# Batch 0 of a routed attention kernel in two rounds of 384 queries, keys and values kept on chip, some splits moved to GpSimd, matmuls on zeros in the first slots

## The chip, the cores and the metric

The kernel runs on one core of one Trainium2 chip. A core has five engines with a queue each: TensorE (PE; its weight loads are listed as PEld), VectorE (DVE), ScalarE (ACT), GpSimd (POOL) and SyncE (SP), which here only issues DMA transfers. Transfers run on 16 DMA engines that all queues share. The metric is the device time of one execution in microseconds; lower is better.

## The reference

Four batches, eight heads, 768 positions of 64 values; 16 centroids a head.

```python
q_n = q / (norm(q) + 1e-6); k_n = ...; c_n = ...
q_assign = argmax(einsum('bhsd,hcd->bhsc', q_n, c_n), -1)
k_assign = argmax(einsum('bhsd,hcd->bhsc', k_n, c_n), -1)
mask = q_assign[:, :, :, None] == k_assign[:, :, None, :]
scores = where(mask, q @ k^T / 8, -1e9)
attn = softmax(scores) @ v
x = attn.transpose(0, 2, 1, 3).reshape(3072, 512)
h = x @ w_in                      # 512 -> 2048
out = (h / (1 + exp(-h))) @ w_out # 2048 -> 512, float32
```

A query sees only the keys that were assigned to its own centroid. The heads' results side by side are the input of a two-layer projection.

## The kernel before

**One head.** `load_qk` and `load_v` (lines 69 to 82) bring a head's q, k and v in as float32, three transfers of 192 KB on SP's queue; POOL casts v into one half of a `vt` tile whose other half is ones, so that the product with `vt` also gives the softmax's sums. `hi` and `lo` (85, 93), both on DVE, split q and k into a float16 part and the float16 rest. `xpose` (101) turns both by DMA transposes into `ab`: 12 tiles (six of q, six of k) of 128 positions, with the high parts on partitions 0 to 63 and the rests on 64 to 127. `logits` (110) are eight matmuls with the centroids; `am_t`, `am_max`, `am_back` (124 to 143) find on DVE the largest of each position's 16 and leave a one-hot code, and `codes` (146) writes the codes, scaled, over partitions 64 to 79 of `ab`. The contraction over 80 partitions in `qk_mm` (158) then gives the score, and a large negative number where the codes differ.

**Slots.** The main loop (386 to 432) runs over the 32 heads i and, in each, over six tiles j of 128 keys. One pair i, j is called a slot here, numbered 6i + j, so that there are 192. In slot i, j PE does the scores of the next slot (768 queries against 128 keys), ACT takes `exp` of this one into `P`, and PE multiplies the head before with its v: `pv_mm` (173), half a pass of 384 queries at a time, three matmuls in each of j = 0, 1, 3, 4. `evac` (182) copies the sums out of PSUM on DVE. The normalization has four steps that are spread over the following two heads: `evac` sends the row of sums out as a small transfer that lays it over partitions (`zt`), `recip` (194) inverts it and writes it to DRAM (`rzd`), `bcast` (202) reads it back to 64 partitions (`rzb`), and `norm` (209), on POOL, multiplies and writes the head's rows of `xt`, the input of the projection.

**Projection.** It is cut in units: `unit_a` (225) is four matmuls for 128 of the 2048 hidden columns and 384 tokens, a tanh on ACT and a product on DVE into `gt`; `unit_aa` (243) is the same for 768 tokens; `unit_b` (267) is 16 matmuls of 512 columns for 128 tokens of output, a copy on DVE and a transfer out. A batch has 32 `unit_a` (or 16 `unit_aa`) and six `unit_b`. All heads of a batch have to be normalized before a `unit_a` of it can run. The batch before's 32 are put in the list `qa` in slot 63, 111 and 159 (head i with i % 8 == 2, j = 3). One is taken in each slot with j = 0, 1, 2, 4, and one `unit_b` in each with j = 5. What is left over, and the whole last batch, runs after the loop.

**What sets the order.** The order of instructions on each engine is the order of the program: nothing is rescheduled, and an engine that waits holds all that is behind it. Loads run ahead of their use by four to six heads. The weights come in eight transfers on POOL's queue (`w_load`, 291), each of which also turns float32 into float16; each is held back by `pace`, a copy on POOL of one column of a certain `P` (line 414). Those stand in heads 2, 4, 6 and 8 (`win_s`) and 9 to 12 (`wout_s`).

## Time and profile before

| | |
|---|---|
| time, median of 3 runs | 398.26 us (397.08 to 400.86) |
| the profiled execution's own time | 396.95 us |
| its span | 395.2 us |
| PE busy | 334.0 us (85%) |
| DVE busy | 264.4 us (67%) |
| ACT busy | 203.8 us (52%) |
| POOL busy | 99.0 us (25%) |
| DMA, hardware queues / POOL's queue | 46.6% / 7.2% of 16 engines' span |
| first exp | 16.1 us |
| first `unit_a` | 96.4 us |

All times in the profile are of one execution. A row of a timeline or a chain gives the start in us, the duration in us, the engine, the line and the operation; brackets give idle time ahead of it and what ended it. A row of a line's view gives the least, median and greatest duration in ns. SPq and POOLq are the engines' issuing of transfers, which isn't counted as busy. In the DMA issues the last number is the median time from issue to landing.

### The profile page before, as it was taken

The page shows a single profiled execution, that of the slowest core. Times are in us where ns is not written, and L with a number is a line of the kernel's source. Part 1 is how long each engine was busy: PE and PEld are TensorE (multiplying, and loading weights), DVE is VectorE, ACT ScalarE, POOL GpSimd, SP SyncE. Part 2 cuts the span into 40 slices and gives each one's busy share as a digit, 9 for nine tenths or more (in the row PEclk, how much of TensorE's full clock was granted, in tenths as well). Part 3 has the DMA queues.
Part 4 walks back from the last instruction along what each step waited for, and adds up shares of the span by engine and source line. Part 5 has one row for each costly group of instructions (what it writes and reads, how often), then busy time and mean ns, then how long its engine had stood idle before and what let it go on. Part 6 is the DMA issues. An engine that isn't in the chain of part 4 may idle for free.

```text
span 395.2 us, 5664 instructions
## 1 busy us (share of the span) xinstructions
PE 334.0 (85%) x1921; PEld 167.8 (42%) x1921; DVE 264.4 (67%) x590; ACT 203.8 (52%) x310; POOL 99.0 (25%) x148
## 2 busy tenths in 40 slices
PE   0539868977598799997999899979999999977995
PEld 0114433433254455553555455445555545443442
DVE  5959967876479977794788877786766345256421
ACT  4237746854376755573666666555657524044300
POOL 3110135454343222223221402260223105000000
PEclk9999978888599999999999999999999999999999
DMA  5695899999979835572555555544311103200022
GB/s 141 172 269 114 188 202 225 186 213 227 128 138 190 207 87 134 133 176 74 148 147 148 122 148 147 143 85 89 88 48 23 47 27 88 80 2 0 0 81 80
DMA packets 82125, 48.84 MB, mean 124 GB/s; under 512 B 62128, under 2 KB 76464, under 8 KB 82096
## 3 DMA queue, kind: packets, MB, share of 16 engines
q1 hardware_dynamic: 79408, 44.29, 46.6%
q0 software_dynamic: 2688, 4.19, 7.2%
q8 instruction: 15, 0.25, 0.3%
q14 instruction: 14, 0.11, 0.1%
HBM read 33.59 MB, written 6.39 MB: 101 GB/s over the span
## 4 chain that ended last, share of the span: by engine, by line
PE 61%; DVE 15%; DMA 12%; ACT 4%; issue 3%; POOL 2%; SPq 2%; ACTq 0%; POOLq 0%; DVEq 0%
PE po L271 21%; PE ph L232 13%; PE pO L177 12%; PE pS L162 7%; DMA vn<-in_v_dram 4%; PE pS L163 3%; PE phs L251 3%; DMA qk<-in_k_dram 3%; DVE osb L186 2%; DMA rzb<-rzd 2%; DMA zt<-osb 2%; DVE gt L261 2%; DVE gt L237 2%; PE psL L116 2%; DVE hl L90 1%
## 5 line engine op out<-in xcount | busy, mean ns | idle before, releaser
L169 ACT ACTIVATE P<-pS 128x768 f16<-128x768 f32 x192 | 148.1, 809 | 37.4 <-PE pS L163 37.2
L177 PE MATMUL pO<-P,vt 128*128 128x384 f16 x384 | 89.1, 344 | 14.0 <-DVE osb L186 13.9
L236 ACT ACTIVATE tn<-ph 128x384 f32<-128x384 f32 x96 | 47.2, 491 | 101.3 <-PE ph L232 96.2
L162 PE MATMUL pS<-ab 80*128 80x512 f16 x192 | 78.8, 410 | 15.5 <-DVE ab L153 9.2
L232 PE MATMUL ph<-xt,win_s 128*128 128x384 f16 x384 | 78.5, 328 | 9.8 <-POOL xt L213 9.8
L271 PE MATMUL po<-wout_s,gt 128*128 128x512 f16 x384 | 85.7, 379 | 0.0
L213 POOL TENSOR_TENSOR xt<-osb,rzb 64x384 f16<-64x384 f32 x64 | 65.1, 1035 | 49.7 <-DMA rzb<-rzd 48.7
L237 DVE SCALAR_TENSOR_TENSOR gt<-tn,ph 128x384 f16<-128x384 f32 x96 | 53.0, 553 | 35.8 <-ACT tn L236 34.0
L82 POOL CAST vt<-vn 128x384 f16<-128x384 f32 x32 | 18.0, 563 | 180.2 <-DMA vn<-in_v_dram 149.6
L177 PEld LDWEIGHTS <-vt 128*128 128x128 f16 x384 | 37.6, 101 | 58.9 <-issue 39.2
L271 PEld LDWEIGHTS <-gt 128*128 128x128 f16 x384 | 37.5, 98 | 43.6
L163 PE MATMUL pS<-ab 80*128 80x256 f16 x192 | 55.6, 289 | 0.0
L276 DVE TENSOR_SCALAR ot<-po 128x512 f32<-128x512 f32 x24 | 16.6, 692 | 52.3 <-PE po L271 52.3
L232 PEld LDWEIGHTS <-win_s 128*128 128x128 f16 x384 | 37.4, 97 | 26.7 <-issue 1.2
L186 DVE COPY osb<-pO 128x384 f32<-128x384 f32 x64 | 35.3, 551 | 3.2 <-PE pO L177 2.9
L96 DVE SCALAR_TENSOR_TENSOR hl<-qk,hl 128x768 f16<-128x768 f32 (+1 forms) x33 | 33.1, 1002 | 0.2
L162 PEld LDWEIGHTS <-ab 80*128 80x128 f16 x192 | 19.8, 103 | 29.0 <-DVE ab L153 10.3
L163 PEld LDWEIGHTS <-ab 80*128 80x128 f16 x192 | 19.8, 103 | 24.5 <-issue 12.8
L251 PE MATMUL phs<-xt,win_s 128*128 128x384 f16 x128 | 22.2, 327 | 5.2 <-DVE gt L261 5.2
L259 ACT ACTIVATE tn<-phs 128x768 f32<-128x768 f32 x16 | 13.0, 811 | 25.0 <-PE phs L251 25.0
L90 DVE TENSOR_SCALAR hl<-qk 128x768 f16<-128x768 f32 (+1 forms) x33 | 19.1, 580 | 8.7 <-DMA qk<-in_k_dram 5.5
L261 DVE SCALAR_TENSOR_TENSOR gt<-tn,phs 128x384 f16<-128x384 f32 x32 | 16.3, 551 | 12.1 <-ACT tn L259 12.1
(45 smaller groups left out, 175.7 us busy)
## 6 DMA issues: line engine op xcount, KB each, us to landing
qk<-in_q_dram SPq DMA_DIRECT2D x32, 192.0 KB, 3.4
qk<-in_k_dram SPq DMA_DIRECT2D x32, 192.0 KB, 3.2
vn<-in_v_dram SPq DMA_DIRECT2D x32, 192.0 KB, 3.7
rzb<-rzd SPq DMA_DIRECT2D x32, 192.0 KB, 3.9
out_dram<-ot SPq DMA_DIRECT2D x24, 256.0 KB, 2.2
win_s<-in_moe_w_in_dram POOLq DMA_DIRECT2D x4, 512.0 KB, 7.9
wout_s<-in_moe_w_out_dram POOLq DMA_DIRECT2D x4, 512.0 KB, 7.5
ab<-hl SPq DMA_TRANSPOSE x33, 3.8
```

Source lines behind the costliest of these rows:

```text
L96: nc.vector.scalar_tensor_tensor(out=hl[:, t, :, 1, :], in0=src[:, t], scalar=QS, in1=hl[:, t, :, 0, :], op0=ALU.mult, op1=ALU.subtract)
L162: nc.tensor.matmul(pS[:, 0:512], lhsT, ab[0:80, 0:4, :].rearrange("p n c -> p (n c)"), start=True, stop=True)
L163: nc.tensor.matmul(pS[:, 512:768], lhsT, ab[0:80, 4:6, :].rearrange("p n c -> p (n c)"), start=True, stop=True)
L169: nc.scalar.activation(out=P, in_=pst.pop((i, j))[:, 0:S], func=AF.Exp, bias=0.0, scale=ESC)
L177: nc.tensor.matmul(pOs[i], vts[i % NV][:, j, :], Ps[i, j][:, c * HALF : c * HALF + HALF], start=(j == 0), stop=(j == NJ - 1))
L186: nc.vector.tensor_copy(osb[:, c * HALF : c * HALF + HALF], pOs.pop(i))
L213: nc.gpsimd.tensor_tensor(out=xts[h // 2][o : o + 64, b * S + c * HALF : b * S + c * HALF + HALF], in0=osbs[i][o : o + 64, cs], in1=rzbs[i ...
L232: nc.tensor.matmul(ph, win_s[:, r, ts(fb, 128)], xts[r][:, T0 : T0 + HALF], start=(r == 0), stop=(r == NR - 1))
L236: nc.scalar.activation(out=tn, in_=ph, func=AF.Tanh, bias=0.0, scale=0.5)
L237: nc.vector.scalar_tensor_tensor(out=gt[:, fb, :], in0=tn, scalar=1.0, in1=ph, op0=ALU.add, op1=ALU.mult)
L251: nc.tensor.matmul(phs[:, 512 * c : 512 * c + HALF], win_s[:, r, ts(fb, 128)], xts[r][:, T0 : T0 + HALF], start=(r == 0), stop=(r == NR - 1),)
L271: nc.tensor.matmul(po, gt[:, fc, ts(t, 128)], wout_s[:, fc, :], start=(fc == 0), stop=(fc == NFB - 1))
```

## The change

Batch 0 is reordered; the later batches keep passes of one head.

- In the first 24 slots, four passes p = 0 to 3 each hold two heads, 2p and 2p + 1, with the first 384 queries: slots 0 to 2 of a pass take two key tiles each of the one head, slots 3 to 5 those of the other. In slots 24 to 47 passes 4 to 7 do the same for the other 384 queries. k (and the first half of q) of the eight heads stay in `abk0` to `abk7`.
- What was the loading, splitting, transposing and routing of one head is that of an *item*. Items 0 to 7 are one head's k and half of its q, nine tiles; items 8 and 9 are the other half of q of four heads each; items 10 to 33 are the heads of batches 1 to 3, twelve tiles.
- Each step of an item stands at a fixed distance from the slot that needs it (`due`, `at`). The steps before slot 0 are run in the order of negative slot numbers.
- `hi` moves from DVE to ACT for items 0 to 3 and to POOL for the others.
- `recip`, `bcast` and `norm` of batch 0's passes stand 3, 5 and 7 slots after the second evacuation, the others 5, 8 and 9 slots, as before.
- The first 16 `unit_a` of batch 0 are put in the list in slot 34, the other 16 in slot 58. In slots 48 to 95 they are taken at j = 1 and 4 alone. The other batches' are put in the list in slots 111 and 159, as before.
- The weights are gated by slots 3, 6, 9 and 12 (`win_s`) and 27, 33, 39 and 45 (`wout_s`).
- `xt` is held for two batches in place of four. `P` has 12 buffers (14), `osb` 3 (4), `rzb` 2 (3), `qk` and `vn` 4 (3).
- `fill` adds matmuls on a tile of zeros into a PSUM tile that nobody reads: 24 ahead of the first work on PE, 4 after the centroids' transpose, 2 in each slot below 34 that isn't a multiple of 3.
- The slots after 191 (to 204) are part of the same loop, where before a tail was written out by hand.

```diff
-    NV = 8
+    NSPLIT = H // 2
...
-    xts = [const.tile([128, NT], f16, name=f"xt{r}") for r in range(NR)]
-    vts = [const.tile([128, NJ, 128], f16, name=f"vt{n}") for n in range(NV)]
+    xts = [[const.tile([128, S], f16, name=f"xt{r}_{n}") for r in range(NR)] for n in range(2)]
+    vts = [const.tile([128, NJ, 128], f16, name=f"vt{n}") for n in range(H)]
...
+    zz = const.tile([128, 512], f16, name="zz")
+    items = [[(h, 0, 0), (h, 0, 3), (h, 1, 0)] for h in range(H)]
+    items += [[(h, 1, 3) for h in range(4 * n, 4 * n + 4)] for n in range(2)]
+    items += [[(hd, 0, 0), (hd, 0, 3), (hd, 1, 0), (hd, 1, 3)] for hd in range(H, NBH)]
+    NI = len(items)
...
+    def head_of(p, s):
+        return (2 * (p % NSPLIT) + s) if p < H else p
...
+    def hi(n, t=None, eng="pool"):
+        if n not in hls:
+            hls[n] = mp.tile([128, 12, 2, D], f16, name="hl", bufs=3)
+        ho, _, src = parts(n, t)
+        if eng == "act":
+            nc.scalar.activation(out=ho, in_=src, func=AF.Copy, bias=0.0, scale=QS)
+        else:
+            nc.gpsimd.tensor_scalar(out=ho, in0=src, scalar1=QS, scalar2=None, op0=ALU.mult)
...
+        if n < H:
+            ab = const.tile([128, 9, 128], f16, name=f"abk{n}")
+        else:
+            ab = mp.tile([128, 12, 128], f16, name="ab", bufs=5)
...
+        p, j = divmod(T, NJ)
+        pS = ps.tile([128, 1024], f32, name="pS", tag="st", bufs=2)
+        if p < H:
+            hd, a = head_of(p, j // 3), 3 * (p // NSPLIT)
+            for t in range(2):
+                nc.tensor.matmul(
+                    pS[:, 512 * t : 512 * t + HALF], k_tile(hd, 2 * (j % 3) + t)[0:80], q_tiles(hd, a, 3),
+                    start=True, stop=True,
                 )
-    @per_head
-    def qk_mm(i, j):
-        ab = abs_[i]
-        pS = ps.tile([128, 1024], f32, name="pS", tag="st", bufs=2)
-        lhsT = ab[0:80, NJ + j, :]
-        nc.tensor.matmul(pS[:, 0:512], lhsT, ab[0:80, 0:4, :].rearrange("p n c -> p (n c)"), start=True, stop=True)
-        nc.tensor.matmul(pS[:, 512:768], lhsT, ab[0:80, 4:6, :].rearrange("p n c -> p (n c)"), start=True, stop=True)
-        pst[i, j] = pS
-    @per_head
-    def exp(i, j):
-        P = mp.tile([128, S], f16, name="P", bufs=14)
-        nc.scalar.activation(out=P, in_=pst.pop((i, j))[:, 0:S], func=AF.Exp, bias=0.0, scale=ESC)
-        Ps[i, j] = P
-    @per_head
-    def pv_mm(i, c, js):
+        else:
+            lhsT = k_tile(p, j)[0:80]
+            nc.tensor.matmul(pS[:, 0:512], lhsT, q_tiles(p, 0, 4), start=True, stop=True)
+            nc.tensor.matmul(pS[:, 512:768], lhsT, q_tiles(p, 4, 2), start=True, stop=True)
+        pst[T] = pS
...
+        P = mp.tile([128, S], f16, name="P", bufs=12)
...
+    def pass_at(p, c):
+        return NJ * p + 3 * c + 3 if p < H else NJ * (p + 1) + 3 * c
...
+        rzb = mp.tile([128, S], f32, name="rzb", bufs=2)
+        rzd = rzds.pop(p)
+        if p < H:
+            for c in range(2):
+                cs = slice(c * HALF, c * HALF + HALF)
+                nc.sync.dma_start(rzb[64 * c : 64 * c + 64, cs], rzd[cs].unsqueeze(0).to_broadcast([64, HALF]))
...
+    def fill(n):
+        if n:
+            junk = ps.tile([128, 512], f32, name="junk", tag="mm", bufs=3)
+            for _ in range(n):
+                nc.tensor.matmul(junk, zz[:, 0:128], zz, start=True, stop=True)
...
+    nc.vector.memset(zz, 0.0)
...
+    at(-3, cast_v, 0)
+    nc.scalar.preload_act_table(AF.Sqrt)
+    fill(24)
...
+    hi(0, None, "act")
+    lo(0)
+    xpose(0)
...
+    fill(4)
...
+    def due(n):
+        if n < H:
+            return 3 * n - 1
+        if n < H + 2:
+            return NJ * (NSPLIT + 2 * (n - H)) - 1
+        return NJ * (n - 2) - 1
+    for n in range(NI):
+        d = due(n)
+        near = n < H + 2
+        at(d - 5, am_back, n)
+        at(d - 5, codes, n)
+        at(d - 6, am_max, n)
+        at(d - 7, am_t, n)
+        at(d - 8, logits, n)
+        if n > 0:
+            x = d - (14 if near else 17)
+            at(x, xpose, n)
+            at(x - 2, lo, n)
+            if n > 1:
+                at(x - 4, hi, n, None, "act" if n < 4 else "pool")
+        if n > 3:
+            at(d - (24 if near else 35), load_qk, n)
+    for hd in range(1, NBH):
+        T = 3 * hd if hd < H else NJ * hd
+        at(T - (12 if hd < H else 15), load_v, hd)
+        at(T - 6, cast_v, hd)
+    for n in range(2 * NR):
+        T = NJ * n // 2 + 3 if n < NR else NJ * (n + 1) - 3
+        def gated(T=T, n=n):
+            nc.gpsimd.tensor_copy(pace, Ps[T][:, 0:1])
+            w_load(n)
+        at(T, gated)
+    on_pe = (logits,)
...
+    pv_at, evac_at, ready = {}, {}, {}
+    for p in range(NBH):
+        for c in range(2):
+            T = pass_at(p, c)
+            pv_at[T] = (p, c, range(0, 3))
+            pv_at[T + 1] = (p, c, range(3, 6))
+            evac_at[T + 2] = (p, c)
+        E = T + 2
+        near = p < H or p == NBH - 1
+        at(E + (3 if near else 5), recip, p)
+        at(E + (5 if near else 8), bcast, p)
+        N = E + (7 if near else 9)
+        for c in range(2):
+            at(N, norm, p, c)
+        if p in (NSPLIT - 1, H - 1):
+            ready[N + 1] = [(0, p // NSPLIT)]
+        elif p % H == H - 1 and p < NBH - 1:
+            ready[N + 1] = [(p // H, 0), (p // H, 1)]
+    for T in range(min(steps), max(steps) + 1):
+        p, j = divmod(T, NJ)
+        if T in ready:
+            qa.extend((*r, fb) for r in ready[T] for fb in range(NFB))
+        qk_mm(T + 1)
+        for f, a in steps.get(T, []):
+            if f in on_pe:
+                f(*a)
+        if T >= 0:
+            wide = H <= p < 2 * H
+            if j in ((1, 4) if wide else (0, 1, 2, 4)):
                 pop_a()
             if j == 5:
                 pop_b()
-            if j in (0, 1):
-                pv_mm(i - 1, 0, range(3 * j, 3 * j + 3))
-            if j in (3, 4):
-                pv_mm(i - 1, 1, range(3 * j - 9, 3 * j - 6))
-            exp(i, j)
-            if j == 0:
-                am_back(i + 1)
-                codes(i + 1)
-                xpose(i + 3)
-                load_qk(i + 6)
-                load_v(i + 5)
-                if i >= 2:
-                    nc.gpsimd.tensor_copy(pace, Ps[i, 0][:, 0:1])
-                    if i % 2 == 0 or i > 2 * NR:
-                        w_load((i - 2) // 2 if i <= 2 * NR else i - NR - 1)
-            if j == 1:
-                hi(i + 5)
-                bcast(i - 3)
-            if j == 2:
-                evac(i - 1, 0)
-                norm(i - 3, 0)
-                norm(i - 3, 1)
-            if j == 3:
-                lo(i + 5)
-            if j == 4:
-                recip(i - 2)
-                am_t(i + 2)
-            if j == 5:
-                evac(i - 1, 1)
-                am_max(i + 2)
-            flush()
-    pop_a()
-    pv_mm(last, 0, range(NJ))
-    flush()
-    pop_a()
-    evac(last, 0)
-    pv_mm(last, 1, range(NJ))
-    recip(last - 1)
-    flush()
-    evac(last, 1)
-    bcast(last - 2)
-    bcast(last - 1)
-    norm(last - 2, 0)
-    norm(last - 2, 1)
-    pop_b()
-    recip(last)
-    flush()
-    bcast(last)
-    for i in (last - 1, last):
-        norm(i, 0)
-        norm(i, 1)
+            if T < 34 and T % 3:
+                fill(2)
+        if T in pv_at:
+            pv_mm(*pv_at[T])
+        exp(T)
+        for f, a in steps.get(T, []):
+            if f not in on_pe:
+                f(*a)
+        if T in evac_at:
+            evac(*evac_at[T])
+        flush()
```

## The prediction

> **What bounds the kernel now.** I read the busy time by stretch of 20 us first (columns: stretch, length, then busy us and instruction count of PE, PEld, DVE, ACT, POOL; granted clock; DMA share, where 1.00 is 16 busy engines; GB/s).
>
> ```profile
> 60.00:80.00 20.00, 17.55 (x108) 8.32 (x108) 16.59 (x40) 14.85 (x20) 8.96 (x11) 0.88 0.99 208
> 80.00:100.00 20.00, 13.55 (x70) 6.15 (x69) 12.24 (x29) 9.29 (x12) 10.81 (x14) 0.80 1.11 211
> 140.00:160.00 20.00, 20.00 (x123) 10.29 (x121) 14.72 (x36) 11.26 (x19) 5.13 (x8) 1.00 0.46 110
> 200.00:220.00 20.00, 19.54 (x124) 10.39 (x122) 16.64 (x36) 13.54 (x22) 5.25 (x8) 1.00 0.65 155
> ```
>
> From 140 us on PE is full. Before 100 us it is not, and the DMA engines are. The chain of work that ended last, cut to that early time, says what is waited for:
>
> ```profile
> 47.22 7.59 DMA zt<-osb
> 59.12 7.18 DMA qk<-in_k_dram
> 87.65 7.19 DMA vn<-in_v_dram
> 95.33 5.18 DMA vn<-in_v_dram
> ```
>
> Each was issued beside a weight load, whose row among the DMA issues gives the time to landing:
>
> ```profile
> win_s<-in_moe_w_in_dram POOLq DMA_DIRECT2D x4, 512.0 KB, 7.9
> ```
>
> The DMA view of 50 to 110 us prices both kinds of traffic in that 60 us:
>
> ```profile
> q1 hardware_dynamic: 18678, 9.13, 76.1%
> q0 software_dynamic: 1536, 2.76, 30.4%
> ```
>
> Software: 0.304 x 60 / 5 weight loads = 3.65 us of the engines each. Hardware: 0.761 x 60 / 8 heads = 5.7 us a head. Together 1.065 of capacity, so this stretch is DMA-bound.
>
> The ACT timeline shows the pace of slots (one exp each; I number slots 6 x head + j):
>
> ```profile
> 46.20 4.59 ACT L169 ACTIVATE P<-pS 128x768 f16<-128x768 f32 x6 [1.11 <-PE pS L163]
> 51.71 2.33 ACT L169 ACTIVATE P<-pS 128x768 f16<-128x768 f32 x3 [0.93 <-PE pS L163]
> 92.92 2.33 ACT L169 ACTIVATE P<-pS 128x768 f16<-128x768 f32 x3 [0.24 <-PE pS L163]
> 104.03 0.80 ACT L169 ACTIVATE P<-pS 128x768 f16<-128x768 f32 x1
> ```
>
> Undisturbed, a head without MoE work takes 51.71 - 46.20 = 5.51 us, and that is DVE: 0.555 (high part) + 0.953 (low part) + 0.546 + 0.343 + 0.358 + 0.575 (argmax) + 4 x 0.251 (codes) + 2 x 0.551 + 0.184 = 5.62. At 104.03 slot 65 starts, one late after a wait of PE's unit_a for xt (6.1 us). From here MoE work fills PE. Slot 96 starts at 152.1 and slot 111, head 18 j=3, at 177.9 by the same timeline.
>
> **The change part by part.** Every unit of work of the projections remains: 96 unit_a, 16 unit_aa, 24 unit_b. What moves is when batch 0's 32 unit_a start: before at slot 64 (first pop after slot 63's extend), now at slot 34, since four passes give the first 384 tokens of all 8 heads. They go on until slot 104, two per six slots in slots 48 to 95 (four elsewhere). From slot 111 on the pops fall in the same slots as before, except that one unit_b, previously after, now falls at slot 107: 3.46 us by its row. So what follows slot 111 costs 395.2 - 177.9 - 3.5 = 213.8 us, and the question is when slot 111 comes.
>
> *To slot 0.* Before 16.1 us. Now logits(2) precedes the first score matmul on PE, and it needs the third transpose. DVE ends the centroid copies at 10.7 in before; two low parts of 0.7 later, at 12.1, that transpose has its data, SP issues it behind two more loads (0.43 each) at about 13, and it lands 3.8 us later by its row, so slot 0 comes at about 18. The first four high parts go to ACT, between its rows of 0.491 (384 columns) and 0.809 (768), which lay idle until 16.14. The 24 zero matmuls begin at about 1.3. The trace has cold and warm rows for 512 columns:
>
> ```profile
> 16.90 0.61 PE L162 MATMUL pS<-ab 80*128 80x512 f16 x1
> 36.60 0.38 PE L162 MATMUL pS<-ab 80*128 80x512 f16 x1
> ```
>
> Start to start that is 0.42 against 0.22. Warm, 24 take 5.3 us and lie in front of the centroid transpose (9.7 us); cold they end at 11.5 and delay it by 1.8. I take 18 and keep 20. The Trainium skill ("TensorE: Matmul & The Clock Gate", Part 1) has the array at half rate until about 3.4 us of sustained work; by it 8 run cold, 16 warm, the end is at about 8.2 us and slot 0 stays at 18; the two rows agree in kind. Inside slots 0 to 33 two zero matmuls stand in two of three slots: 0.29 us a slot warm. PE's own slot is then 0.32 + 0.33 + 0.06 + 0.29 = 1.0 us, below what follows; without cover they cost 46 x 0.22 = 10 us, cold twice that.
>
> The exp of two halves of 384 has the row of the tanh of that shape (0.811 against 0.809), the score matmuls keep 768 columns, and the split loads and broadcasts keep their bytes: nothing.
>
> *Slots 0 to 33.* DVE: an item of nine tiles costs 0.953 x 0.75 + 0.546 + 0.343 + 0.358 + 0.575 + 3 x 0.251 = 3.29, its high part having gone to ACT (four items) and POOL; with about six items, three low parts more and four evacuations in slots 0 to 15, some 19 us there, then less than PE's 1.0 a slot: 18 + 19 + 18 = 55. DMA: K, V and half of Q of all heads, then the other halves, make 8 heads. Of a head's 5.7 us I give 0.9 to rzb (one of four equal 192 KB transfers) and the two small ones, an estimate; so 8 x 4.8 + 4 passes x 0.9 + about 4 for batch 1's first item = 46, plus four win loads, now gated by slots 3, 6, 9, 12, 14.6: 61 us. The first 20 us of before carry 0.63 x 20 = 12.6; the other 48 at 1.065 take 45.6. So slot 34 at 66, **DMA-bound**; bounds 58 (DVE and PE with some slack) and 72 (the 6.1 us wait for xt again: recip, bcast and norm have only 3, 2 and 2 slots, and POOL, SP and DVE each stand in order behind their wait). Before, slot 34 was at 60.4: this stage loses about 6.
>
> *Slots 34 to 50.* Three wout loads remain: per six slots 5.7 + 3.65 = 9.35, over 1.065 = 8.8 us; DVE needs 5.07 + 4 x 0.553 = 7.3. 17 slots: 21 to 25, I take 24. Slot 51 at 90 (before 78.1).
>
> *Slots 51 to 95.* A pass on DVE: 5.62 - 0.555 + 2 x 0.553 = 6.2; PE: the period of 10.6 us in the full stage,
>
> ```profile
> 141.19 3.46 PE po L271 x16
> 151.78 3.46 PE po L271 x16
> ```
>
> less 3.46 and four unit_a of 0.65 leaves 4.54, plus two unit_a 5.8. High parts on POOL are unseen in before. Below: nothing, DVE's 0.555 simply goes. Price on POOL: the cast of 384 columns 0.507, doubled 1.0; the product of two inputs, 0.994, doubled 2.0; I take 1.0, the one-input row. Either fits POOL's pass (1.0 + 0.5 + 2.0 of 6.6). What it does to DVE is the danger:
>
> ```profile
> L135 DVE TENSOR_TENSOR oh<-LT,mx x32: 357/358/1132, 13.4 to 299.6; 128x192 f16<-128x192 f32 x32
> L151 DVE TENSOR_SCALAR ab<-ohT x64: 250/251/1057, 14.4 to 300.9; 16x384 f16<-16x384 f16 x64
> ```
>
> The long ones lie beside POOL work. At worst one pass gains 0.77 + 4 x 0.81 + 0.66 (low part, 953 to 1609) = 4.7; medians are untouched with POOL at 0.25 to 0.5 busy. I take 0.4: 6.6 a pass. The skill ("GPSIMD Engine Reference", 4.1 and 8) speaks against the move: elementwise work belongs on VectorE, and instructions with two SBUF inputs contend with POOL; if that held every low part to its longest, 0.66 x 7.5 would add 5 us. Three of these passes carry a unit_b: PE 5.8 + 3.46 = 9.3. Sum: 4.5 x 6.6 + 3 x 9.3 = 58 (bounds 56 and 76). Slot 96 at 148 against 152.1.
>
> *Slots 96 to 110.* 7.3 + 6.7 + (3.46 + 2.3) = 20, before 25.8: at this point batch 0's projections are nearly done. Slot 111 at 168.
>
> In the full stage DVE has 5.07 + 4 x 0.553 + 0.69 = 8.0 of 10.6, so POOL's high parts may stretch it by 2.6 a head for nothing. Smaller rings (P 12 for 14, osb 3 for 4, rzb 2 for 3) are freed a slot or more before they are rewritten: nothing. The end: pops 9 and 2 in the slots after 191, norm of the last head some 19 us after them by its waits (2.0 + 2.8 + 3.9 landings, 2.0 norm, 9 to the second evacuation and the reciprocal), PE has 1.9 + 11 x 0.65 + 4 x 3.46 = 22.9 to cover it; if not covered, 3.
>
> **Sum.** 168 + 213.8 = 382 span. Around the span lie 396.95 - 395.2 = 1.75: 384. The profiled execution is 1.3 under the median of 398.26, which I compare with; one per cent (4 us, about what a measurement tells here) lies at 394.3 and 402.2.
>
> **Rivals.**
> 1. *The transfers overlap better than their sum.* DVE and PE pace alone: slot 34 at 58, 20 for the next 17, 56, 20, 213.8, 1.75: 369. For it: loads run 24 to 35 slots ahead. Against: 1.065 was the ceiling of 60 us.
> 2. *POOL's port takes DVE's gain.* At three of the 4.7 in the passes without unit_b (4.5 x 2.6 more), 1.5 in the others, and slot 34 at 70: 384 + 12 + 4 = 400 at most, 395 in the middle. For: the 1132. Against: the medians.
> 3. *Slower: the weights in front.* Eight loads fall in slots 3 to 45, where reads are densest and zt, rzd and rzb have least slack. If each holds everything for its 7.6 us to landing, not 3.65, eight x 3.95 = 32 come on top less what stalls hid already: 403 to 415. It decides from 5.9 us a load (18 us over). For: the four 5 to 7.6 us links of the chain. Against: the 46.7 us of slots 24 to 63 held four loads at a loss of about 11 in all.
> 4. *The change doesn't do what it says:* unit_a at slot 34 waits on xt and PE cools, or zeros leave the clock cold: 386 to 391, in the forecast's range.
>
> **Chances.** Forecast (376 to 392, with 4) 0.54; rival 1 0.14; rival 2 0.18; rival 3 0.14. Range 369 to 402: it takes in rivals 1 and 2. Faster by over 1%: 0.54 + 0.14 + a little of 2 = 0.70; within 1%: 0.15; slower: 0.15.
>
> **What would show it.** First unit_a at about 66, against 96; slot 111 at 168; DMA share near 1.0 until 90; the full stage at 10.6 a head. If slot 34 comes after 80 or a head in the full stage takes over 11, I am wrong.

## The result, and the profile after

The changed kernel takes **423.94 us** (median of 4 runs, 418.38 to 429.61), the one before 398.37 (397.08 to 400.86). The ratio, taken here and below over the executions within 1.5% of each kernel's fastest, is **1.0533**, 95% interval 1.0424 to 1.0643: some 5% slower, where 384 us were forecast. The profiled execution took 418.38 us, with a span of 416.2.

The starts of the slots (one `exp` each, from ACT's timeline) show where it went. "Rest" is what follows slot 111. The last four rows are kernels of the next section. Every row is one execution.

| us | slot 0 | 34 | 51 | 96 | 111 | rest | span |
|---|---|---|---|---|---|---|---|
| before | 16.1 | 60.4 | 78.1 | 152.1 | 177.9 | 217.2 | 395.2 |
| predicted | 18 | 66 | 90 | 148 | 168 | 213.8 | 382 |
| after | 17.4 | 76.8 | 106.6 | 171.5 | 193.2 | 223.0 | 416.2 |
| c2, five edits | 18.2 | 68.1 | 92.8 | 157.3 | 183.1 | 213.1 | 396.2 |
| c5, c2 with high parts on POOL | 18.6 | 71.6 | 101.2 | 167.6 | 194.2 | 213.2 | 407.4 |
| c7, c2 with short distances | 17.3 | 70.8 | 104.2 | 167.5 | 193.5 | 213.1 | 406.6 |
| c8, c2 with the early start | 18.6 | 68.9 | 99.6 | 168.9 | 191.5 | 221.1 | 412.6 |

Stage by stage, after minus predicted: -0.6 to slot 0, +11.4 in slots 0 to 33, +5.8 in 34 to 50, +6.9 in 51 to 95, +1.7 in 96 to 110, +9.2 in the rest; 34.4 in all.

First the busy time by stretch of the kernel after (columns as in the prediction):

```profile
40.00:60.00 20.00, 13.82 (x73) 6.70 (x73) 11.46 (x28) 8.46 (x11) 7.06 (x7) 0.83 0.65 154
60.00:80.00 20.00, 13.09 (x65) 6.24 (x64) 6.60 (x14) 8.26 (x11) 9.66 (x10) 0.83 0.72 137
200.00:220.00 20.00, 19.50 (x97) 9.48 (x97) 10.80 (x25) 8.79 (x15) 7.62 (x8) 0.85 0.31 73
```

From 40 to 80 us no engine is full and neither are the DMA engines (0.65 and 0.72; before they stood at 0.99 in both stretches). DVE, 15.8 and 16.6 of 20 us busy before, is now at 11.5 and 6.6. Nothing is the bound there: everything waits for something in turn. The last row looks full, but its clock of 0.85 says that PE works there for longer, not on more.

The chain of work that ended last, cut to 17 to 120 us, has these transfers among its pieces (start, duration, transfer):

```profile
33.80 5.92 DMA zt<-osb
41.62 6.71 DMA rzd<-rz
...
64.10 6.45 DMA zt<-osb
...
90.79 4.07 DMA rzd<-rz
```

They carry 1.5 and 3 KB; the median of `zt<-osb` from issue to landing is 2.4 us between 20 and 110 us, that of `rzd<-rz` 1.7. They are two of the links of the normalization. Before, both were slower there, 3.6 and 6.2 us by the median, but more slots stood between the steps. Of the loads of q, k and v, which took pieces of 5 to 7 us before, one piece of 2.42 us is left. DVE's timeline shows what stands behind one of them, and PE's what stands behind DVE:

```profile
70.57 0.19 DVE L273 RECIPROCAL rz<-zt 128x6 f32<-128x6 f32 x1 [5.02 <-DMA zt<-osb]
70.68 0.52 DVE L258 COPY osb<-pO 128x384 f32<-128x384 f32 x1
```

```profile
71.25 1.12 PE L252 MATMUL pO<-P,vt 128*128 128x384 f16 x3 [4.90 <-DVE osb L258]
...
77.33 0.65 PE L314 MATMUL ph<-xt,win_s 128*128 128x384 f16 x3
80.06 0.32 PE L314 MATMUL ph<-xt,win_s 128*128 128x384 f16 x1 [2.07 <-POOL xt L296]
```

The reciprocal stands on DVE ahead of the evacuation (L258); it waits 5.02 us for 1.5 KB, the evacuation with it, and PE 4.90 us for the bank. The last two rows are the first `unit_a`: three of its matmuls run at 77.33, the fourth waits for the norm of the last pass, with all of PE behind it. The same three waits over the whole run, in the table of waits of the kernel after (engine and line, releaser: us in all, times, longest):

```profile
POOL xt L296 <- DMA rzb<-rzd: 115.9, 22, 9.6
...
PE pO L252 <- DVE osb L258: 23.5, 19, 5.4
...
DVE rz L273 <- DMA zt<-osb: 18.0, 5, 5.2
```

Before:

```profile
POOL xt L213 <- DMA rzb<-rzd: 48.7, 11, 11.7
PE pO L177 <- DVE osb L186: 13.9, 15, 2.9
DVE rz L196 <- DMA zt<-osb: 8.0, 3, 3.4
```

POOL's part is on the page of the kernel after, among the busy times and the costliest groups:

```profile
PE 353.1 (85%) x1993; PEld 175.0 (42%) x1993; DVE 265.3 (64%) x567; ACT 205.0 (49%) x313; POOL 152.1 (37%) x156
...
L296 POOL TENSOR_TENSOR xt<-osb,rzb 64x384 f16<-64x384 f32 x64 | 63.8, 1010 | 168.4 <-DMA rzb<-rzd 115.9
...
L138 POOL TENSOR_SCALAR hl<-qk 128x768 f16<-128x768 f32 (+1 forms) x30 | 62.9, 2098 | 14.9 <-DVE ohT L190 8.9
```

A high part takes 2.1 us on POOL, where 1.0 was taken, and 0.555 on DVE before. DVE hardly waits for it in this kernel:

```profile
DVE hl L143 <- POOL hl L138: 1.8, 2, 1.0
```

PE's 353.1 us hold 24.2 us of zeros. Up to slot 111 PE is without work for some 41 us, before for 43 (the time to its first matmul and the gaps between them, from the trace): since the zeros now fill part of that time, useful work waits for longer than before.

### The profile page after: what moved, and what is told of

Its sections match the earlier page's. It is cut to its first block, busy times and chain, and to the rows that moved or that the text cites. A ratio compares the mean times of both kernels' runs of the same rounds, so it can differ in the third digit from the quotient of the medians.

```text
span 416.2 us, 5850 instructions
## 1 busy us (share of the span) xinstructions
PE 353.1 (85%) x1993; PEld 175.0 (42%) x1993; DVE 265.3 (64%) x567; ACT 205.0 (49%) x313; POOL 152.1 (37%) x156
## 3 DMA queue, kind: packets, MB, share of 16 engines
q0 software_dynamic: 2688, 4.19, 6.4%
## 4 chain that ended last, share of the span: by engine, by line
PE 48%; DMA 16%; DVE 16%; POOL 5%; SPq 5%; issue 5%; ACT 4%; POOLq 0%; DVEq 0%; ACTq 0%
PE po L353 18%; PE ph L314 10%; PE pO L252 8%; DMA rzb<-rzd 5%; DMA zt<-osb 5%; PE pS L220 4%; PE phs L333 3%; DMA rzd<-rz 3%; POOL hl L138 3%; DVE gt L319 3%; DMA abk<-hl 2%; POOL xt L296 2%; DVE ab L202 2%; PE pS L221 2%; SPq L108 2%
## 5 line engine op out<-in xcount | busy, mean ns | idle before, releaser
L296 POOL TENSOR_TENSOR xt<-osb,rzb 64x384 f16<-64x384 f32 x64 | 63.8, 1010 | 168.4 <-DMA rzb<-rzd 115.9
L252 PE MATMUL pO<-P,vt 128*128 128x384 f16 x384 | 88.0, 340 | 23.7 <-DVE osb L258 23.5
L353 PE MATMUL po<-wout_s,gt 128*128 128x512 f16 x384 | 88.1, 387 | 0.0
L138 POOL TENSOR_SCALAR hl<-qk 128x768 f16<-128x768 f32 (+1 forms) x30 | 62.9, 2098 | 14.9 <-DVE ohT L190 8.9
L220 PE MATMUL pS<-ab 80*128 80x512 f16 x144 | 56.0, 389 | 9.9 <-ACT P L235 9.3
L358 DVE TENSOR_SCALAR ot<-po 128x512 f32<-128x512 f32 x24 | 16.6, 691 | 58.8 <-PE po L353 58.8
L221 PE MATMUL pS<-ab 80*128 80x256 f16 x144 | 39.6, 275 | 0.0
L258 DVE COPY osb<-pO 128x384 f32<-128x384 f32 x64 | 35.0, 546 | 4.0 <-PE pO L252 4.0
L143 DVE SCALAR_TENSOR_TENSOR hl<-qk,hl 128x768 f16<-128x768 f32 (+1 forms) x34 | 30.5, 899 | 4.5 <-ACT hl L136 2.4
L377 PE MATMUL junk<-zz 128*128 128x512 f16 x72 | 24.2, 455 | 1.2 <-DVE zz L390 1.2
L221 PEld LDWEIGHTS <-ab 80*128 80x128 f16 x144 | 14.4, 100 | 23.4 <-issue 14.3
L343 DVE SCALAR_TENSOR_TENSOR gt<-tn,phs 128x384 f16<-128x384 f32 x32 | 16.3, 550 | 12.1 <-ACT tn L341 12.1
```

Source lines behind the costliest of these rows:

```text
L138: nc.gpsimd.tensor_scalar(out=ho, in0=src, scalar1=QS, scalar2=None, op0=ALU.mult)
L220: nc.tensor.matmul(pS[:, 0:512], lhsT, q_tiles(p, 0, 4), start=True, stop=True)
L221: nc.tensor.matmul(pS[:, 512:768], lhsT, q_tiles(p, 4, 2), start=True, stop=True)
L252: nc.tensor.matmul(pOs[p, c], vts[hd % H][:, j, :], rhs, start=(j == 0), stop=(j == NJ - 1))
L258: nc.vector.tensor_copy(osb[:, c * HALF : c * HALF + HALF], pOs.pop((p, c)))
L296: nc.gpsimd.tensor_tensor(out=xts[b % 2][h // 2][o : o + 64, T0 : T0 + HALF], in0=osbs[p][o : o + 64, cs], in1=rzbs[p][o : o + 64, cs], op ...
```

## The experiments

A diff is against the changed kernel unless it says otherwise, and expectations are as they were put down. Where two kernels ran on different chips, their ratios to the kernel before on the same chip are compared. Two theories stood at first: **A**, POOL's slow high parts hold it back; **B**, the normalization's steps stand too close together and each waits for a transfer that is late beside the weight loads.

### One cause at a time

**e1: the high parts on DVE.**

```diff
-            nc.gpsimd.tensor_scalar(out=ho, in0=src, scalar1=QS, ...)
+            nc.vector.tensor_scalar(out=ho, in0=src, scalar1=QS, ...)
```

> The changed kernel with one part undone: the high parts of items 4 to 33 are made on DVE again, not on POOL. Theory A (POOL): one high part takes 2.1 us on POOL, and there it stands between a norm, which waits for rzb, and the low part, whose transpose stands on SP ahead of the next rzb, so a head cannot go faster than that loop of some 10 us. Then slots 51 to 110 fall from 86.6 us to about 72 and what follows slot 111 from 223 to about 214: 423.9 becomes 400 to 406. Theory B (short chain beside weights): the loss sits in slots 0 to 50, where DVE stands before zt; nothing there changes, and DVE has 0.55 us more a head: 420 to 428.

416.69 us, ratio 1.0515 (1.0440 to 1.0591). Theory A alone falls: the ratio hardly moves (the two intervals leave room for some 6 us), and slots 51 to 95 take 63.8 us, in the kernel after 64.9. The chain of this kernel there is a round trip (start, duration, piece):

```profile
120.05 0.65 PE pO L252 x3
...
121.02 0.67 PE ph L314 x4
...
121.71 0.49 ACT tn L318
122.20 0.71 ACT P L235
122.91 0.54 DVE gt L319
123.45 0.47 DVE hl L138
123.92 0.48 DVE osb L258
...
124.44 0.65 PE pO L252 x3
```

`unit_a` at j = 1 and 4 stands just behind the half pass; its tanh and product come ahead of the evacuation, for which the next half pass waits: 4.39 us from one `pO` to the next, two to a head.

**e2: recip, bcast and norm of batch 0 at 5, 8 and 9 slots.**

```diff
-        near = p < H or p == NBH - 1
+        near = p == NBH - 1
```

> The changed kernel with batch 0's reciprocal, broadcast and norm at 5, 8 and 9 slots after the evacuation, as in the other batches, in place of 3, 5 and 7; the first unit_a then come in slot 36. Theory B: DVE's five waits for zt (18.0 us in all) lose about 2.5 us each, SP's waits for rzd vanish: slot 51 at about 94 in place of 106.6, 410 to 414 in all. Theory A: the loop through POOL decides from slot 51 on and is untouched, but the gain in front of it remains, so A alone gives 420 to 426 only if the early waits come back elsewhere.

423.46 us, 1.0664 (1.0578 to 1.0750). B alone falls as well: no gain.

**e7: the four `wout_s` loads in slots 52, 55, 58 and 61.**

```diff
-        T = NJ * n // 2 + 3 if n < NR else NJ * (n + 1) - 3
+        T = NJ * n // 2 + 3 if n < NR else 52 + 3 * (n - NR)
```

> The changed kernel with the four loads of the second weight gated by slots 52, 55, 58 and 61 in place of 27, 33, 39 and 45; the first unit_b needs them in slot 71. Theory B: zt and rzd of passes 3 to 7 no longer lie beside a weight load and land in about 2 and 2.8 us, not 4 to 6.5: slot 51 at about 95 in place of 106.6, of which the later loads take back up to 5 in slots 52 to 70: 412 to 418. Theory A: no change beyond that, slots 51 to 110 stay at 86 or more. If the loads cost their share wherever they stand, 422 to 426.

424.73 us, 1.0725 (1.0657 to 1.0793). Moving these four gains nothing. The three loads of slots 6, 9 and 12 stayed where they were.

**e11: all eight loads seven slots apart.**

```diff
-        T = NJ * n // 2 + 3 if n < NR else NJ * (n + 1) - 3
+        T = 3 + 7 * n
```

> The changed kernel with the eight weight loads seven slots apart, gated by slots 3, 10, 17, ... 52, in place of 3, 6, 9, 12 and 27, 33, 39, 45. Theory D: no three of them meet any more, the transpose and the small transfers beside them wait for one load (some 7 us to landing) and not for three: slot 51 at 95 to 100 in place of 106.6, 410 to 416. If it is the bytes and not their burst, slot 51 stays at 104 or more and the time at 419 to 425.

424.78 us, 1.0705 (1.0638 to 1.0772). Spreading them brings nothing by itself: slot 34 comes at 73.3, earlier than in the kernel after, but slots 34 to 50 then take 36.2 us, not 29.8.

**e10: no weight loads.** Both weights are constants that POOL writes (1.8 us each of the eight), so the projection is computed with other weights; the 4.19 MB are left out.

```diff
-            nc.gpsimd.dma_start(win_s[:, n, :], moe_w_in[ts(n, 128), :])
+            nc.gpsimd.memset(win_s[:, n, :], 0.01)
...
-            nc.gpsimd.dma_start(
-                wout_s[:, 4 * r : 4 * r + 4, :],
-                moe_w_out[512 * r : 512 * r + 512, :].rearrange("(c p) d -> p c d", p=128),
-            )
+            nc.gpsimd.memset(wout_s[:, 4 * r : 4 * r + 4, :], 0.01)
```

> The changed kernel without the eight weight loads: each is replaced by a fill of the same tile with a constant on POOL, some 2.2 us each, so the projections are computed with constant weights. Theory D (burst of weight loads): the loss in slots 0 to 50 comes from the 4.2 MB of weights, three of whose first four loads start within 6 us and hold the transfers queued behind them (transposes took 9 to 21 us to land there, 3.8 elsewhere). Then slot 51 comes at 80 to 88 in place of 106.6, and the time is 395 to 405. Theory B (the chain of normalization is too short by itself): zt and rzd still hold DVE and SP, slot 51 at 95 or later, 412 or more.

406.76 us, 1.0255 (1.0193 to 1.0317); slot 34 at 65.6, slot 51 at 95.6. The loads hold 11 us: by slot 51 (106.6 to 95.6), and by the ratios (0.028 of 396; the intervals allow 5 more or less). That is all of them, not just their place. With the same short distances DVE's waits for `zt` up to slot 34 shrink from 16.0 us to 4.0. But even with none, the kernel is 2.5% slower than the one before *with* its loads, and the head of the first `unit_a` (slots 30 to 35) takes 13.1 us.

**e3: no zeros.**

```diff
-    fill(24)
...
-    fill(4)
...
-            if T < 34 and T % 3:
-                fill(2)
```

> The changed kernel without any of the 72 matmuls on zeros (24 in front, 4 after the centroids, 44 in slots below 34), which nothing reads. Theories A and B both put the loss elsewhere: PE waits in those slots, so 421 to 426, or 2 to 4 slower if the clock stays at half rate longer. A third theory, C: the 24 in front and those in the slots delay PE's own work; then slot 34 comes 5 us or more earlier and the time is 414 to 419.

425.85 us, 1.0612 (1.0485 to 1.0739), an interval that covers the changed kernel's ratio: the zeros don't cost the loss, and whether they help is settled further down.

**e12: units of slots 48 to 95 at j = 2 and 5.**

```diff
-            if j in ((1, 4) if wide else (0, 1, 2, 4)):
+            if j in ((2, 5) if wide else (0, 1, 2, 4)):
```

> The changed kernel with the unit_a of slots 48 to 95 taken at j = 2 and 5 in place of j = 1 and 4. Theory E (round trip): in those slots a half pass is one round from PE over the tanh on ACT and the product on DVE to the evacuation, which stands behind that product on DVE and for which PE's next pass waits, 3.9 to 4.4 us each; with the product behind the evacuation the round is broken: slots 51 to 95 take 58 us in place of 64.9, 412 to 418. Theory A (POOL's loop of norm, high part, transpose and broadcast): no change, 64 or more there.

421.57 us, 1.0564 (1.0484 to 1.0644). Slots 51 to 95 take 60.1 us: the round trip was real, for some 4 us in that stage (60.1 again in c1 below, which has the same edit; 63.4 or more in all other single edits), but the total didn't follow.

**e13: the first 16 `unit_a` in slot 42.**

```diff
-            ready[N + 1] = [(0, p // NSPLIT)]
+            ready[N + 1 if p >= NSPLIT else 42] = [(0, p // NSPLIT)]
```

> The changed kernel with the first 16 unit_a of batch 0 put in the list in slot 42 in place of 34; nothing else moves. Theory F (the early start itself): in slot 34 PE stands in order before xt, whose chain of three small transfers and two waits needs some 15 us from the evacuation in slot 26, and eight slots are not that long; besides, batch 0's units then end at slot 104 and PE has nothing until xt of batch 1 (slots 105 to 112). Then slots 30 to 35 fall from 15.8 to about 9 us, the pause at slots 108 to 113 (14.8) to about 11, and the time from 423.9 to 411 to 416. If the wait is only moved, since DVE, SP and POOL stand before the same transfers: 420 or more.

417.08 us, 1.0521 (1.0459 to 1.0584). In the total a miss, but one term came in exactly: the rest after slot 111 is **213.1 us**, as predicted (213.8), not 223.0. What the 9.9 us are can be seen in PE's timeline of the kernel after,

```profile
195.99 0.65 PE L314 MATMUL ph<-xt,win_s 128*128 128x384 f16 x3
200.50 0.48 PE L314 MATMUL ph<-xt,win_s 128*128 128x384 f16 x1 [3.85 <-POOL xt L296]
...
202.37 5.40 PE L353 MATMUL po<-wout_s,gt 128*128 128x512 f16 x16
```

against that of e13:

```profile
203.59 3.62 PE L353 MATMUL po<-wout_s,gt 128*128 128x512 f16 x16
```

With the start in slot 34, batch 0's units run out at slot 104. The slots up to 111 then hold only attention, but for a `unit_b` in slot 107, and most pass in 0.8 us or so; the norm that batch 1's first `unit_a` needs stands a fixed number of *slots* behind, and comes 3.85 us late. PE has cooled by then: the granted clock is 0.67 from 202 to 208 us, 1.00 in e13 from 203 to 208, and `unit_b` takes 5.40 us in place of 3.62. Started eight slots later, the units reach as far as slot 112, and there is no gap.

### Together, and one taken back

**c1: e1, e11 and e12 together.**

```diff
-            nc.gpsimd.tensor_scalar(out=ho, in0=src, scalar1=QS, ...)
+            nc.vector.tensor_scalar(out=ho, in0=src, scalar1=QS, ...)
...
-        T = NJ * n // 2 + 3 if n < NR else NJ * (n + 1) - 3
+        T = 3 + 7 * n
...
-            if j in ((1, 4) if wide else (0, 1, 2, 4)):
+            if j in ((2, 5) if wide else (0, 1, 2, 4)):
```

> The three edits together: high parts on DVE, the weight loads seven slots apart from slot 3 on, and the unit_a of slots 48 to 95 at j = 2 and 5. If the parts add, 423.9 less 5 (measured for the high parts), 10 and 7: 400 to 404. If one of D and E is wrong, 410 or more.

413.81 us, 1.0442 (1.0365 to 1.0520). Not what was hoped for: the head of the first `unit_a` now takes 19.1 us.

**c2: the longer distances and the later start added, loads nine slots apart.** Against c1:

```diff
-        T = 3 + 7 * n
+        T = 3 + 9 * n
...
-        near = p < H or p == NBH - 1
+        near = p == NBH - 1
...
-            ready[N + 1] = [(0, p // NSPLIT)]
+            ready[N + 1 if p >= NSPLIT else 42] = [(0, p // NSPLIT)]
```

> High parts on DVE, weight loads nine slots apart (3, 12, ... 66), the unit_a of slots 48 to 95 at j = 2 and 5, batch 0's reciprocal, broadcast and norm at 5, 8 and 9 slots, its first unit_a in slot 42. If the four causes (POOL, weights, round trip, early start) add, as e10 and c1 let expect: slot 34 at 68, slot 51 at 93, slot 96 at 152, slot 111 at 178, 394 to 402: no slower than before. If there is a cost in the two rounds as such (nine-tile items, 1.5 times the transfers a slot), 406 or more.

**396.70 us** (10 runs), 1.0002 (0.9962 to 1.0041). The whole loss is gone. What is left of the change, the two rounds, keys and values on chip, the smaller rings and ACT's four high parts, neither gains nor costs in sum.

**c3: c2 without the zeros.** The diff is that of e3.

> The kernel c2 without any matmul on zeros. The zeros took 24.2 us of PE in the changed kernel. Theory C: some of that delays PE's own work: 4 to 8 us under c2. If PE waits for DVE and the transfers there anyway, within 3 us of c2.

395.83 us, 0.9994 (0.9961 to 1.0026): within the measurement the zeros bring and cost nothing. This is what e3 left open.

Then four of c2's five edits were taken back, each by itself.

**c5: the high parts back on POOL** (diff against c2).

```diff
-            nc.vector.tensor_scalar(out=ho, in0=src, scalar1=QS, ...)
+            nc.gpsimd.tensor_scalar(out=ho, in0=src, scalar1=QS, ...)
```

> The combination (396.7) with one of its edits taken back: the high parts of items 4 on are on POOL again. If the causes add, this one gives back its own share: DVE's stretches (26 us against 13 in all, a part of them on the path) and POOL's 2.1 us a part in the loop rzb, norm, cast, high part, low part, transpose: 401 to 405. If one cause hides behind the others and only all four gone makes the gain, it gives back nearly everything: 410 or more. If POOL's part costs nothing once there is distance between recip, bcast and norm: 395 to 399.

409.57 us, 1.0372 (1.0318 to 1.0427). Three timelines of c5 show one case. POOL:

```profile
77.74 2.06 POOL L296 TENSOR_TENSOR xt<-osb,rzb 64x384 f16<-64x384 f32 x2 [8.61 <-DMA rzb<-rzd]
79.89 2.13 POOL L138 TENSOR_SCALAR hl<-qk 128x768 f16<-128x768 f32 x1
```

DVE, whose low part needs that high part:

```profile
82.05 0.96 DVE L143 SCALAR_TENSOR_TENSOR hl<-qk,hl 128x768 f16<-128x768 f32 x1 [4.83 <-POOL hl L138]
...
83.58 0.55 DVE L258 COPY osb<-pO 128x384 f32<-128x384 f32 x1
```

And PE:

```profile
84.18 1.12 PE L252 MATMUL pO<-P,vt 128*128 128x384 f16 x3 [4.01 <-DVE osb L258]
```

The norm stands ahead of the high part on POOL and waits 8.61 us for `rzb`; the high part waits with it, the low part (L143) waits on DVE, the evacuation behind that, and PE 4.01 us for the evacuation. In c5's table of waits that is

```profile
DVE hl L143 <- POOL hl L138: 21.6, 7, 6.8
```

and c2, whose high parts are on DVE, has no such wait. The second cost is on DVE itself. The rows of the codes, c5's first,

```profile
L200 DVE TENSOR_SCALAR ab<-ohT x56: 250/254/1395, 45.2 to 312.5; 16x384 f16<-16x384 f16 x56
```

and c2's,

```profile
L200 DVE TENSOR_SCALAR ab<-ohT x56: 250/254/552, 47.5 to 301.5; 16x384 f16<-16x384 f16 x56
```

have the same medians and another longest. Summed over all lines, what DVE's instructions take beyond their line's median is 26.1 us in c5 and 12.1 in c2 (27.1 in the kernel after, 14.1 in e1, 13.5 before). So the 30 high parts save DVE about 16 us and their neighbours give some 14 of them back. How the loss, 14.7 us by the ratios, divides between the wait and the stretch is open.

**c6: the weights' gates back** (diff against c2).

```diff
-        T = 3 + 9 * n
+        T = NJ * n // 2 + 3 if n < NR else NJ * (n + 1) - 3
```

> The combination (396.7) with the weights gated again in slots 3, 6, 9, 12, 27, 33, 39 and 45. If the causes add: slot 24 later by 5 to 8 us than the combination's 52.4 (item 8's transpose lands beside three loads), slot 51 by 8 to 10, and 402 to 408. If hidden behind the others: 410 or more. If the weights' place is not a cause, as the three single trials of it would have it: 395 to 399.

398.18 us (10 runs, 390.71 to 405.17), 0.9947 (0.9887 to 1.0006). That ratio rests on the four fastest of the ten; the medians of all give 398.18 / 396.11 = 1.0052. Either way the place of the loads costs at most some 2 us once the other four edits are in; the spread is wide. One cost of theirs is still there: a transpose of 14.1 us, for which PE waits 6.0 us in slots 12 to 23 of the profiled execution. Slot 96 comes at 156.0 all the same (157.3 in c2).

**c7: the short distances back** (diff against c2).

```diff
-        near = p == NBH - 1
+        near = p < H or p == NBH - 1
```

> The combination (396.7) with recip, bcast and norm of batch 0's passes back at 3, 5 and 7 slots. DVE waits again for zt and POOL for rzb, about 5 us each time that a load or a transpose is beside it. If the causes add: slots 24 to 51 longer by 3 to 6 us and 400 to 404; hidden: 410 or more; no cause: 395 to 399.

409.02 us, 1.0246 (1.0154 to 1.0337; 1.0326 by the medians of all). In c7's DVE timeline

```profile
81.45 0.19 DVE L273 RECIPROCAL rz<-zt 128x6 f32<-128x6 f32 x1 [10.32 <-DMA zt<-osb]
```

and in PE's

```profile
82.14 1.12 PE L252 MATMUL pO<-P,vt 128*128 128x384 f16 x3 [9.21 <-DVE osb L258]
```

the reciprocal, two slots earlier than in c2, waits 10.32 us, and PE 9.21. In c2 no reciprocal between 50 and 110 us waited longer than 3.8 us.

**c8: the start of the units right behind the norm, here slot 36** (diff against c2).

```diff
-            ready[N + 1 if p >= NSPLIT else 42] = [(0, p // NSPLIT)]
+            ready[N + 1] = [(0, p // NSPLIT)]
```

> The combination (396.7) with the first 16 unit_a in the list right after the norm of pass 3 (slot 36 by the longer distances) and not in slot 42. PE then stands at the first unit_a, and batch 0's units run out by slot 106, so that heads 18 and 19 take 14 and 12 us (8.5 and 10.6 in the combination). If the causes add: slot 51 later by 2 to 6 us, what follows slot 111 220 in place of 213, sum 404 to 410. If only the early wait counts and the late gap is filled: 398 to 402.

412.46 us, 1.0388 (1.0314 to 1.0461). Both ends of it are there: the first `unit_a`,

```profile
70.91 0.65 PE L314 MATMUL ph<-xt,win_s 128*128 128x384 f16 x3
78.29 0.48 PE L314 MATMUL ph<-xt,win_s 128*128 128x384 f16 x1 [6.73 <-POOL xt L296]
78.56 1.17 PE L252 MATMUL pO<-P,vt 128*128 128x384 f16 x3
```

waits 6.73 us and leaves PE cold (1.17 us for three `pO`, 0.65 warm), and the rest after slot 111 is 221.1 us, near the 223.0 of the kernel after.

**What the set says.** Any one of three things, POOL's high parts, the short distances or the early start, put back into a kernel that ties costs 10 to 15 us by its ratio: some 40 us added up, where the whole loss is 21. And each one alone taken out of the changed kernel gives back 1 us or less by its ratio, with intervals that leave room for some 6. So they are not terms of a sum; they lengthen or tighten the same ring of waits, and while one is left, the ring stays late. This ring is argued from the chains of c5, c7 and c8; the runs show the counts. Two questions are without a measurement: c2 with the pops at j = 1 and 4 again, and c2 with every high part on ACT.

### The one part in the old order

**b1: the kernel before with the high parts of heads 5 to 31 on POOL.** Against the kernel before:

```diff
-        nc.vector.tensor_scalar(out=hl[:, t, :, 0, :], in0=src[:, t], scalar1=QS, ...)
+        (nc.gpsimd if i > 4 else nc.vector).tensor_scalar(out=hl[:, t, :, 0, :], in0=src[:, t], scalar1=QS, ...)
```

> The kernel before with one part of the change alone: the high parts of heads 5 to 31 on POOL (2.1 us each there) at the same places. Theory A's remainder, from e1 (5 to 7 us for 30 of them): 400 to 404, the loss in heads without unit_b and in the early heads, where DVE paces. If POOL's port costs nothing where PE is full and DVE's 0.55 a head pays in the early heads: 392 to 397.

**525.02 us**, 1.3238 (1.3167 to 1.3309): a miss by 120 us, and the most telling run. Its chain from 137 us on (start, duration, piece), one head:

```profile
137.81 4.21 DMA vn<-in_v_dram
142.17 0.50 POOL vt L82
142.78 0.83 issue
143.61 2.16 POOL hl L90
145.79 2.69 DVE hl L96
...
150.10 1.30 SPq L106
151.46 1.04 SPq L72
152.55 0.43 SPq L73
153.03 5.01 DMA vn<-in_v_dram
```

Three engines that each run in order close a ring. POOL's high part stands behind a cast that waits for a load of v; DVE's low part waits for POOL; SP's transposes (L106) wait for DVE; and the next load of v stands behind them on SP. The low part is slow as well: it takes 2.69 us beside the norm that follows the high part on POOL, where its median is 0.96:

```profile
L96 DVE SCALAR_TENSOR_TENSOR hl<-qk,hl x33: 558/959/2694, 4.4 to 390.5; 128x768 f16<-128x768 f32 x31, 128x384 f16<-128x384 f32 x2
```

Once around takes 153.03 - 137.81 = 15.2 us; a head takes 13.6 in slots 51 to 95 of b1 (102.3 us for seven and a half), and 9.9 before. `load_v` issues the load and its cast together, so that POOL always stands for the landing (149.6 us of it already before), which is free only as long as nobody waits for POOL. The arithmetic alone would be 2.16 us for 0.555, on an engine that was three quarters idle.

## Why the prediction was wrong

*To slot 0* held: 17.4 against 18. The first 24 zeros took 7.02 us, between 24 x 0.22 = 5.3 warm and 24 x 0.42 = 10.1 cold (in the slots there are 44 more, not 46). High parts on ACT take 0.68 us, between the 0.491 and 0.809 that bounded them.

***Slots 0 to 33* is the step that failed first.** It called the stretch "DMA-bound" and summed bytes, a weight load as 3.65 us: slot 34 at 66, bounds 58 and 72. It came at 76.8, past the bound, and at 75.9 to 84.3 in e1, e3, e7, e12 and e13, which have the same first four loads and the same distances. The DMA share is 1.05 from 20 to 40 us, as reckoned, but 0.65 and 0.72 in the next 40, so bytes don't set it. What the runs put in its place is when transfers land beside the loads: without the loads (e10) and with the same distances slot 34 comes at 65.6. The step had the right words for what waits, "recip, bcast and norm have only 3, 2 and 2 slots, and POOL, SP and DVE each stand in order behind their wait", and priced them once, at "the 6.1 us wait for xt again". They are paid every pass: transfers of 1.5 and 3 KB at 5 to 7 us, DVE behind them (3.9, 5.3, 1.9 and 5.0 us for `zt` in the four passes of this stretch), PE behind DVE. Nor did 5 or 8 slots help alone (e2): there DVE waits for `zt` once, 4.0 us, but a transpose takes 17.0 us beside the loads and PE waits 9.0 us for it.

*Slots 34 to 50* was 29.8 us, not 24, and the forecast again summed bytes. It holds the first `unit_a`. In c2, which starts them in slot 42 and has the other four edits too, it is 24.7; in c8, c2 with the early start, 30.7.

*Slots 51 to 95* was 64.9, not 58, inside the bounds of 56 and 76 but for another reason than the one bounded. The price "I take 1.0, the one-input row" is 2.13 us, above the upper end of 2.0: the nearest row was a plain cast, and a multiplication by a constant takes twice that for a column. The rule that spoke against the move (the Trainium skill, "GPSIMD Engine Reference", 8: GpSimd shares its SBUF interfaces with VectorE) agrees with the runs: beside POOL's high parts DVE's instructions lengthen by 13 to 14 us in all, though mostly the small code writes and not the low parts that the step reckoned with (their excess is 0.8 us). What the step had no term for is the *wait* for POOL, in order behind its norm (21.6 us in c5, but 1.8 in the kernel after). So POOL didn't pace the passes in the kernel after: e1 takes 63.8 there. The round trip through `unit_a`, tanh, product and evacuation did (4.39 us a half pass; e12 60.1, near the 58 of the sum). It isn't all that can: c2, with the same pops and the later start, takes 64.5, and what paces it there is open.

The Trainium skill ("GPSIMD Engine Reference", 4.1) calls elementwise operations with one input roughly line-rate on GpSimd. The measured 2.13 us against 0.555 on DVE for the same 128x768 is 3.8 times as long; for this instruction the measurement decides.

*Slots 96 to 110* was 21.7 for 20.

"What follows slot 111 costs 213.8" failed by 9.2, and was right where its condition holds: 213.0 to 213.4 in all six kernels with the start in slot 42 (e13, c2, c3, c5, c6 and c7), 219.6 to 223.0 in the ten others that have the two rounds. The step counted that "batch 0's projections are nearly done" as a gain and didn't ask what PE does until batch 1's first row of `xt` is there: it stands and cools.

**The rivals.** Number 3, *the weights in front*, had the sign and part of the mechanism. Its price was 32 us; the loads are worth 11 us (e10), and their place next to nothing once the other four edits are in (c6). Number 2, POOL's port, is there in size (14 us of DVE's 16 gone), but it was priced as the whole of POOL's part, and its 395 to 400 left out the waits. Number 4, "unit_a at slot 34 waits on xt and PE cools", happened as written, at 386 to 391; in c8 that alone, with the gap it leaves at slot 105, is 15 us over c2. The test was the right one: "If slot 34 comes after 80 or a head in the full stage takes over 11, I am wrong". Slot 34 came at 76.8, heads 18 and 19 take 14.8 and 12.6.

And where was the gain that was forecast? Its source was batch 0's `unit_a`, started in slot 34 and not 64: slots 51 to 95 were to gain 16 us on before, 96 to 110 another 6, the rest 3.4, for 12 lost up to slot 51. In c8 the units are started right behind the norm, and PE stands there; what is done early is missing at slot 105. With the start in slot 42 (c2) slots 51 to 95 gain 9.5 (64.5 us), 96 to 110 nothing (25.8, as before), the rest 4.1, and slot 51 comes 14.7 later: a tie.

## What to carry to other kernels

Where engines run in order, a distance between two steps that is counted in loop iterations is a distance in time only as long as iterations keep their length: check it again, against the sum of the links (here three transfers in a row, of 3 to 7 us when loads are about, in e13 one of 12.2), whenever a change makes the iterations shorter. An instruction moved to an idle engine inherits every wait ahead of it in that engine's queue, and hands it to all who need its result; look there first, at the engine's busy share last. When several causes tighten one ring, taking one out shows nothing; put each back into a version that has none of them.

## What the runs showed of the hardware that was not expected

- Scaling 128x768 from f32 to f16 takes 2.13 us on POOL, 0.555 on DVE; the cast on POOL takes 0.507 for 384 columns, about half as much per column.
- A DMA transpose (that of item 8) issued at 34.38 us beside three weight loads of 512 KB wasn't in until 43.59 in the kernel after. The same one took 10.4 to 21.0 us in the seven other kernels with loads in slots 6, 9 and 12 (e7: from 34.27 to 51.15), 3.7 to 7.3 in those with loads seven or nine slots apart, 3.7 without loads (e10); the median of all transposes is about 3.8. What holds a transpose behind the loads is open.
- The kernel after and e13 are the same program up to slot 33, and yet slots 12 to 23 took 21.6 us in the one's profiled execution and 31.4 in the other's. That transpose is most of it: it took 20.1 us in e13, and PE waits 10.8 us for it there (the row below, from e13's table of waits up to 67 us); the kernel after has no such wait of PE. So up to slot 34 one execution differs from the next by some 8 us (76.8 and 84.3), and a stage's figure of a single execution is good to no more than that; the verdicts rest on the timed ratios.

```profile
PE psL L161 <- DMA ab<-hl: 10.8, 1, 10.8
```

- POOL's scaling lengthens DVE's small writes beside it, from 0.25 to as much as 1.40 us (1.06 before, beside the norm on POOL). In b1 it is the low parts beside the norm that lengthen, from 0.96 to as much as 2.69 us.
- Zeros on PE made no measurable difference: 1.0002 with, 0.9994 without.
